# Converting half of a later stage's weights one stage earlier, and passing them through DRAM

## The chip, the cores and the metric

The kernel runs on one core of a Trainium2 chip. The metric is the time of one execution on the device in microseconds (us), the median of several runs. The core's engines are TensorE (PE, with its weight loads shown as PEld), VectorE (DVE), ScalarE (ACT), GpSimd (POOL) and SyncE (SP), which issues nearly all DMAs of this kernel. Each engine works its own queue strictly in order.

## The reference, cut to what matters

```python
x = causal_attention(q, k, v, s)        # 4 batches x 8 heads x 576 positions x 64 -> 2304 tokens x 512
r = maximum(x @ w_in, 0)                # 512 -> 2048          first MLP
x = (s * (r * r) + b) @ w_out           # 2048 -> 512
h = maximum(maximum(x @ w1, x @ w2), x @ w3)   # 512 -> 768 each   second MLP
out = h @ w_out2                        # 768 -> 512
```

The inputs of the second MLP (w1, w2, w3, w_out2) arrive in 64-bit floats. Every product is worked out from operands that are split in a high and a low part ("hi", "lo"), by three TensorE matmuls (L247, L248, L249 of the kernel before).

## The kernel before, in words

There are four stretches.

**Attention and A, 0 to about 345 us.** Attention for 20 jobs runs beside the first half of the first MLP's hidden units ("A"). A goes through eight pieces of tokens, (b, hf) with 320 columns (hf 0) or 256 (hf 1). For each piece come eight "up" products (by `f`, four chunks of 512 inputs each), a relu on DVE (L985), a square and a high part on ACT (L989, L236), a low part on POOL (L243), then four "down" products `e` in two pairs, each left by DVE (`leave`, L1041) into a tile `ya` that SP stores to DRAM (`y0_d`). The attention results (`x_copy`, L614, on DVE) are split for A and also stored to DRAM (`x_d`).

**A alone, about 345 to 432 us.** Attention has ended; the down products of piece (2,0) and the pieces (2,1), (3,0) and (3,1) are left. Until `begin_2` the up and down products share two PSUM banks (ring `mm`); from `begin_2` on there are eight (`mm8`). `begin_2` also frees the attention's memory, so that SP can load the weights of the second half (`wb_in`, `wb_out`, eight loads of 512 KB each, from a DRAM copy `wb_d` that was made earlier) and the first inputs `xs` (`load_x`, from `x_d`; two buffers, split by ACT L1078 and DVE L1080 into `xbh`, `xbl`).

**B, about 432 to 644 us.** The second half of the hidden units, in six groups of 384 tokens: eight up products, relu, square, hi, lo (`gbh`, `gbl`), four down products. `leave` (L1072) adds the first half's result `y0` and writes a tile `y` (ring of two), which SP stores to `y_d`. Beside it the weights of the second MLP are converted, in six "quads": (matrix i, half kk) for w3, w2 and w1. A quad is four pieces of 128 x 384. Each piece is loaded (`wst`, 384 KB, ring of three), scaled on ACT (L1115) and rebuilt as a 32-bit float by four operations and an addition on DVE (L1120, L1122, L1124, L1126, L1102); then come the sums of Strassen's method (`ts`, ring of two), and seven high parts on ACT and seven low parts on DVE (L1099) into the tiles `sw`. The converted w3 is stored to DRAM (21 stores of 256 KB) so that its tile can take w1.

**Stage 3, about 644 us to the end.** The second MLP by the seven products of the Strassen-Winograd method, for four groups of tokens (halves of 320 or 256 columns) and nine units each (three weights times three column blocks `p`). The operand tiles `ty` are made from `y_d` (loads `bl`, shifts on ACT, sums on DVE with the ring `ts`). The weights of w3 are loaded from DRAM again for each unit (`load_s`, L1272, 84 loads of 256 KB, five buffers, shown as `rest`; DRAM tensor `s_d`). When a group is done, the last products (`last`, L247 to L249 on `wf` and `h`, 512 columns) are copied out of PSUM by ACT (`store`, L1372) into the one tile `o` (shown as `rest`), and SP stores it to `out`.

A planner (`Plan`) puts all steps in order when the program is built, from needs, rings of buffers, priorities and its own costs. On the chip each engine then works through its list in that order: a step that waits holds all that stand behind it on its engine, and SP's DMA issues too are such a list.

The lines that set when a quad's piece may start, before:

```python
            g, f = divmod(int(z * PACE_S), NB)       # PACE_S = 1.7, NB = 8
            start = needs + [("middle_2",), ("after", ("upb", g, 0, f, 0))]
```

`middle_2` comes when A's last step is done; `("upb", g, 0, f, 0)` is B's up product f of group g.

## Time and profile before

| | |
|---|---|
| median of three runs | 937.21 us (934.38, 937.21, 939.47) |
| the profiled execution: its time, its span | 938.2 us, 936.4 us |
| mean granted TensorE clock, of full speed | 0.978 |
| busy share: PE, PEld, DVE, ACT, POOL | 95%, 89%, 68%, 54%, 36% |

The span runs from the first to the last recorded instruction; the 1.8 us between it and the time lie around it. A busy share is over the whole span. Times below are microseconds from the span's start. A row of a timeline gives start, duration, engine, line, operation, written tile and read tiles, and in brackets how long the engine had been idle before and what released it. The program's names in rows are those of the trace, where some DRAM tensors and tiles go by a shared name: `y_d` stands for `y_d` and `y0_d`, `rest` for all that is cut from one area in stage 3.

### The profile page before, as it was taken

What the parts mean: (1) busy time and instruction counts of PE and PEld (TensorE: products, weight loads), DVE (VectorE), ACT (ScalarE), POOL (GpSimd) and SP (SyncE); (2) the same over time, 40 slices, a digit from 0 to 9 for tenths busy, and PEclk for the clock granted to TensorE, in tenths of its full rate; (3) what the DMA queues carried; (4) which work ended last, traced back from release to release, by engine and by line L of the source; (5) the groups of instructions that cost most, each with busy time, mean ns of one, the idle gap of its engine ahead of it and who ended that gap; (6) DMA issues with size and microseconds to landing.
All of it is one profiled execution on the core that took longest, in us unless ns stands there. A gap on an engine that the chain in (4) does not pass through costs nothing.

```text
span 936.4 us, 17708 instructions
## 1 busy us (share of the span) xinstructions
PE 891.6 (95%) x6088; PEld 829.6 (89%) x6088; DVE 636.0 (68%) x1623; ACT 505.1 (54%) x1320; POOL 340.4 (36%) x388
## 2 busy tenths in 40 slices
PE   4899899999999999999999999998999999999996
PEld 4677798988888999999999899998998898998995
DVE  7698978887788422224975977948995575765570
ACT  4688699999877733232452553555344344233231
POOL 3344457656554243222331331233233232342220
PEclk8699999999999999999999999999999999999999
DMA  7446365775664101912369244235342343242331
GB/s 237 135 142 193 120 194 184 213 221 159 198 192 160 43 25 55 380 40 91 120 192 280 90 148 138 93 102 186 119 151 87 113 142 117 81 131 94 113 102 45
DMA packets 96841, 131.72 MB, mean 141 GB/s; under 512 B 9200, under 2 KB 61680, under 8 KB 96752
## 3 DMA queue, kind: packets, MB, share of 16 engines
q1 hardware_dynamic: 96656, 130.45, 43.9%
q8 instruction: 48, 0.79, 0.3%
q14 instruction: 41, 0.34, 0.1%
q10 hardware_dynamic: 96, 0.15, 0.0%
HBM read 97.21 MB, written 33.36 MB: 139 GB/s over the span
## 4 chain that ended last, share of the span: by engine, by line
PE 46%; DVE 8%; DMA 7%; issue 3%; ACT 2%; POOL 1%; SPq 0%; ACTq 0%; DVEq 0%; POOLq 0%
PE mm L247 15%; PE mm L248 15%; PE mm L249 15%; DMA wst<-in_moe_w_dram 2%; DMA xs<-x_d 1%; DVE g L985 1%; DMA out_dram<-rest 1%; DVE sw L1099 1%; DMA wb_in<-wb_d 1%; DMA rest<-s_d 1%; DMA y<-y_d 1%; DVE wst L1126 1%; DVE bl L1122 1%; PE px L609 1%; DVE wst L1124 1%
## 5 line engine op out<-in xcount | busy, mean ns | idle before, releaser
L989 ACT ACTIVATE g<-g 128x384 f32<-128x384 f32 (+2 forms) x112 | 53.5, 478 | 115.6 <-DVE g L985 115.5
L1302 DVE TENSOR_TENSOR rest<-mm,rest 128x320 f32<-128x320 f32 (+1 forms) x156 | 70.2, 451 | 58.8 <-ACT rest L1329 42.2
L243 POOL TENSOR_TENSOR gbl<-g,gbh 128x384 fp32r<-128x384 f32 x48 | 55.7, 1161 | 144.4 <-ACT gbh L236 139.1
L247 PE MATMUL mm<-ty,sw 128*128 128x320 f32 (+1 forms) x336 | 99.8, 297 | 4.7 <-ACT rest L1372 2.9
L248 PE MATMUL mm<-ty,sw 128*128 128x320 f32 (+1 forms) x336 | 99.7, 297 | 0.7 <-DVE ty L1099 0.7
L249 PE MATMUL mm<-ty,sw 128*128 128x320 f32 (+1 forms) x336 | 99.4, 296 | 0.0
L590 PE MATMUL pt<-ident,pp 128*128 128x128 f32 x480 | 80.7, 284 | 15.0 <-ACT pt L236 10.7
L985 DVE TENSOR_SCALAR g<-mm 128x384 f32<-128x384 f32 (+2 forms) x112 | 55.3, 495 | 54.8 <-PE mm L249 48.8
L549 ACT ACTIVATE pp<-pp,mn 128x192 f32<-128x192 f32 (+4 forms) x160 | 88.8, 559 | 2.8 <-DVE mn L543 2.7
L243 POOL TENSOR_TENSOR set<-raw,set 64x1152 fp32r<-64x1152 f32 x24 | 65.1, 2712 | 62.9 <-ACT set L472 45.5
L243 POOL TENSOR_TENSOR ga<-g,ga 128x320 fp32r<-128x320 f32 (+1 forms) x64 | 53.8, 843 | 87.6 <-ACT ga L236 84.6
L247 PE MATMUL mm<-xhi,wa_in 128*128 128x320 f32 (+1 forms) x256 | 79.6, 311 | 1.3 <-DVE ya L1041 1.3
L247 PE MATMUL mm<-ga,wa_out 128*128 128x320 f32 (+2 forms) x256 | 80.0, 312 | 0.1
L236 ACT ACTIVATE pt<-pt 128x256 f32<-128x256 f32 (+3 forms) x181 | 72.7, 428 | 11.9 <-PE pt L590 10.7
L249 PE MATMUL mm<-ga,wa_out 128*128 128x320 f32 (+2 forms) x256 | 76.4, 298 | 2.7 <-DVE wa_out L291 2.7
L590 PEld LDWEIGHTS pt<-ident,pp 128*128 128x128 f32 x480 | 56.9, 143 | 24.8 <-ACT pt L236 12.4
L248 PE MATMUL mm<-ga,wa_out 128*128 128x320 f32 (+2 forms) x256 | 76.3, 298 | 0.9 <-POOL ga L243 0.8
L248 PE MATMUL mm<-xlo,wa_in 128*128 128x320 f32 (+1 forms) x256 | 75.8, 296 | 0.2 <-POOL xlo L243 0.2
L543 DVE CUSTOM_DVE_ANT_0 pp<-late_keys,ps 64x64 f32<-64x64 f32 (+4 forms) x160 | 63.2, 420 | 18.7 <-PE ps L532 11.1
L1102 POOL TENSOR_TENSOR rest<-rest 128x320 f32<-128x320 f32 (+1 forms) x48 | 40.8, 857 | 96.7 <-DVE rest L1302 61.7
L249 PE MATMUL mm<-xhi,wa_in 128*128 128x320 f32 (+1 forms) x256 | 75.8, 296 | 0.0
L248 PE MATMUL mm<-gbl,wb_out 128*128 128x384 f32 (+1 forms) x192 | 66.2, 345 | 4.2 <-POOL gbl L243 4.2
(218 smaller groups left out, 2778.1 us busy)
## 6 DMA issues: line engine op xcount, KB each, us to landing
rest<-s_d SPq DMA_DIRECT2D x84, 256.0 KB, 3.1
wst<-in_moe_w_dram SPq DMA_DIRECT2D x24, 384.0 KB, 3.6
raw<-in_q_dram SPq DMA_DIRECT2D x24, 288.0 KB, 4.2
raw<-in_k_dram SPq DMA_DIRECT2D x24, 288.0 KB, 3.3
wb_d<-wbs SPq DMA_DIRECT2D x21, 256.0 KB, 2.5
s_d<-sw SPq DMA_DIRECT2D x21, 256.0 KB, 3.2
xs<-x_d SPq DMA_DIRECT2D x24, 192.0 KB, 3.7
y<-y_d SPq DMA_DIRECT2D x24, 192.0 KB
```

The costliest lines, as they stand in the source:

```text
L236: nc.scalar.activation(dst, src, AF.Copy, scale=1.0 if scale is None else scale)
L243: ENGINES[on].tensor_tensor(dst, a, b, op=ALU.subtract)
L247: nc.tensor.matmul(ps, lhs[0], rhs[0], start=first, stop=False)
L248: nc.tensor.matmul(ps, lhs[0], rhs[1], start=False, stop=False)
L249: nc.tensor.matmul(ps, lhs[1], rhs[0], start=False, stop=last)
L543: nc.vector.tensor_tensor_reduce(out=pp[j][i][:n, k0:k1], in0=late_keys[:n, a:a + k1 - k0], in1=ps_.pop((job.n, u, j))[:n, :k1 - k0], scal ...
L549: nc.scalar.activation(p[:n, :w], p[:n, :w], AF.Exp, bias=mns[job.n, j][:n, i:i + 1], scale=-1.0, accum_out=sums[job.n % 2][:n, j, i:i + 1])
L590: nc.tensor.transpose(pt[:, c - c0, :], pp[j][i][:, c * P:(c + 1) * P], ident)
L985: nc.vector.tensor_scalar(st["g", f], st["u", f][:, :n], 0.0, None, op0=ALU.max)
L989: nc.scalar.activation(st["g", f], st["g", f], AF.Square)
L1102: ENGINES[on].tensor_tensor(dst, a, b, op=ALU.add)
L1302: add(key(name), "DVE", dve_ps(n), prio(), pr(x) + needs, lambda: nc.vector.tensor_tensor(dst(), ps(x), tmp(z), op=ALU.add))
```

## The change

- Three of the six quads, (w3, kk 0), (w3, kk 1) and (w2, kk 0), are converted while A runs alone: their loads may go from `begin_2` on, as A's matmul steps pass certain `marks`. Their high and low parts go to a ring of ten tiles `sd` in memory that later holds `wb_out`, and from there to DRAM (21 stores of 384 KB, tensors `s_d`). (w2, kk 0) is loaded back into `sw` at `middle_2` by seven loads. The other three quads stay in B, with `PACE_S` 3.2 in place of 1.7.
- `begin_2` no longer waits for the last copies of the attention, whose tiles move to a pool of their own (`axp`). So it comes earlier; the eight banks come later, by a step of their own (`banks_2`) behind the last `x_copy`.
- The loads of `wb_in` keep their place behind `begin_2`; those of `wb_out` wait for `middle_o`, when all 21 stores from `sd` are issued.
- `load_s` in stage 3 reads its 256 KB from the `s_d` tensors as they were stored by quad. A run of bytes without a gap on the DRAM side is now 128 elements (512 bytes); it was 512 elements (2 KB).
- B's result tile `y` no longer has a ring of its own but takes the ring `ts` of two, which the Strassen sums of both B and stage 3 use. `y0` takes tiles of `axp`.
- `store` copies into the ring `wst` of three tiles in place of the single `o`, and the DMA to `out` is a step of its own on SP.
- `h` and `tmp` tiles are housed elsewhere, without another operation.

```diff
-WO = ((0, 1, 2), (3, 4), (5, 6, 7))
-PACE_S = 1.7
+WO = ((0, 1, 2), (3, 4, 5), (6, 7))
+SD = (4, 4, 2)
+PACE_S = 3.2
...
-        if att:
+        if att and key[0] not in ("copy_rb", "x_copy", "x_hi", "x_lo"):
             attention.append(key)
...
     def begin_2():
-        phase[0] = 2
         right.close()
...
+    def middle_o():
+        tiles = [late["rwo"].tile([P, 2, len(fs), DM], F32R, name=f"wb_out{z}", tag=f"wo{z}") for z, fs in enumerate(WO)]
...
+    def banks_2():
+        phase[0] = 2
+
+    add(("banks_2",), "", 0.0, 0, [("after", ("x_copy", job.n, hf)) for job in jobs for hf in job.halves], banks_2)
...
-            y = late["sp"].tile([P, G2], F32, name="y", tag=tag("y"))
+            y = late["st2"].tile([P, G2], F32, name="y", tag=tag("ts"))
...
-        nc.sync.dma_start(late["swp"][z].bitcast(F32), s3_d[i // 3][x])
+        p = i // 3
+        nc.sync.dma_start(late["swp"][z].rearrange("p (k n) -> p k n", n=P).bitcast(F32), s_d[1][x][:, :, p * P:(p + 1) * P])
...
+    def save_s(q, x):
+        nc.sync.dma_start(s_d[q[0] - 1][x][:, 2 * q[1]:2 * q[1] + 2], sds[q, x].bitcast(F32))
+
+    def load_sw(kk, x):
+        nc.sync.dma_start(late["sw"][1][:, x, :, kk, :].bitcast(F32), s_d[0][x][:, 2 * kk:2 * kk + 2])
+
+    def window(y):
+        return lambda x: [("begin_2",), ("after", marks[int((4 * y + x) * len(marks) / 15)])]
...
+    STAGED = ((2, 0), (2, 1), (1, 0))
+    for y, (i, kk) in enumerate(STAGED):
+        convert_quad(y, i, (w1, w2, w3)[i], kk, window(y))
...
     def store(g, j):
-        o = late["o"]
+        o = late["st2"].tile([P, DM], F32, name="o", tag=tag("wst"))
...
-            add(("store", g, j), "ACT", act_ps(DM), next_prio(FIRST), [("last", g, j, f)], store, g, j, take=[("o", [("store", g, j)])])
+            add(("store", g, j), "ACT", act_ps(DM), next_prio(FIRST), [("last", g, j, f)], store, g, j, take=[("wst", [("out", g, j)])])
+            add(("out", g, j), "SP", (1, DM), next_prio(FIRST), [("store", g, j)], leave_o, g, j)
```

The order of TensorE's work is the same in both kernels, and the other engines' orders agree up to `begin_2`. Three places show what moves.

DVE, from the attention's last `x_copy` of 320 columns to the relus of piece (2,1), before (`ya<-mm` are the four leaves of piece (2,0)):

```order
L614 TENSOR_TENSOR x_0_4923<-px,rb_4914 128x320
L1041 TENSOR_SCALAR ya<-mm,s_sb 128x320 x4
L985 TENSOR_SCALAR g<-mm 128x256 x8
L614 TENSOR_TENSOR x_1_5188<-px,rb_4739 128x256
L1041 TENSOR_SCALAR ya<-mm,s_sb 128x256
```

The same stretch after the change:

```order
L616 TENSOR_TENSOR x_4940<-px,rb 128x320
L1087 TENSOR_TENSOR xbl_4938<-xs_4936,xbh_4937 128x384
L1087 TENSOR_TENSOR xbl_4944<-xs_4942,xbh_4943 128x384
L1043 TENSOR_SCALAR ya<-mm,s_sb 128x320
...
L1087 TENSOR_TENSOR xbl_4989<-xs_4987,xbh_4988 128x384
L1106 TENSOR_TENSOR sd_4926<-bl,sd_4926 128x384
L1087 TENSOR_TENSOR xbl_5009<-xs_5007,xbh_5008 128x384
L1127 TENSOR_SCALAR bl<-bl 128x384
L1129 SCALAR_TENSOR_TENSOR bl<-wst,bl 128x384
L1131 TENSOR_SCALAR wst<-bl 128x384
L1133 SCALAR_TENSOR_TENSOR wst<-wst 128x384
L1043 TENSOR_SCALAR ya<-mm,s_sb 128x320
```

The third leave of the piece, the last row, now stands behind the splits of all four input chunks and behind most of two pieces of a quad.

SP's DMA issues there, after the change:

```order
L1069 DMA xs_4936<-x_d 128x384
L1069 DMA xs_4942<-x_d 128x384
L1113 DMA wst<-in_moe_w_dram 128x384
L628 DMA x_d<-x_4940 128x320
L1059 DMA wb_in<-wb_d_72 128x2x512
L1059 DMA wb_in<-wb_d_73 128x2x512
L1059 DMA wb_in<-wb_d_74 128x2x512
L1059 DMA wb_in<-wb_d_75 128x2x512
L1059 DMA wb_in<-wb_d_76 128x2x512
L1069 DMA xs_4987<-x_d 128x384
L1113 DMA wst<-in_moe_w_dram 128x384
L1044 DMA y_d<-ya 128x320
```

The third input chunk (`xs_4987`, read by the third `xbl`) is issued behind five loads of `wb_in`; the fourth comes in the row after these. Before, the same sequence, without the `wst` loads, stood some 25 us later, where A had eight banks.

DVE at the passage from B to stage 3 (`y` are leaves of B's last group, `ts` and `ty` the first operands of stage 3), before:

```order
L1072 SCALAR_TENSOR_TENSOR y<-mm,s_sb,y_7973 128x384
L285 TENSOR_SCALAR wst<-wsa 128x256 x2
L1072 SCALAR_TENSOR_TENSOR y<-mm,s_sb,y_7987 128x384
L1099 TENSOR_TENSOR ts<-bl 128x320
L287 SCALAR_TENSOR_TENSOR wst<-wst 128x256
L1099 TENSOR_TENSOR ts<-bl,ts 128x320
```

The same place after the change:

```order
L1079 SCALAR_TENSOR_TENSOR y<-mm,s_sb,y_7839 128x384
L1106 TENSOR_TENSOR ty<-bl,ty 128x320
L1079 SCALAR_TENSOR_TENSOR y<-mm,s_sb,y_7843 128x384
L1106 TENSOR_TENSOR ts<-bl,ts 128x320
...
L1079 SCALAR_TENSOR_TENSOR y<-mm,s_sb,y_7971 128x384
L286 TENSOR_SCALAR wst<-wsa 128x256
L282 SCALAR_TENSOR_TENSOR wsa<-wst,wsa 128x256
L1079 SCALAR_TENSOR_TENSOR y<-mm,s_sb,y_7987 128x384
L1106 TENSOR_TENSOR ts<-bl 128x320
L288 SCALAR_TENSOR_TENSOR wst<-wst 128x256
L1106 TENSOR_TENSOR ts<-bl,ts 128x320
```

The order is nearly the same, but `y` and `ts` now take turns on the same two tiles: a `ts` that follows a `y` in a tile has to wait until SP has stored that `y`. In the upper four rows the second `ts` of kk 0 (`t2`) has also moved: it now follows both leaves of the first pair, which it preceded.

## Rows read from the trace of the kernel before

**Rows 1.** The page's busy times, shares of the span and instruction counts

```profile
PE 891.6 (95%) x6088; PEld 829.6 (89%) x6088; DVE 636.0 (68%) x1623; ACT 505.1 (54%) x1320; POOL 340.4 (36%) x388
```

**Rows 2.** Windows of B: busy (x) PE, PEld, DVE, ACT, POOL; clock, DMA, GB/s

```profile
440.00:460.00 20.00, 19.71 (x113) 19.25 (x112) 19.86 (x38) 12.56 (x32) 10.67 (x15) 1.00 0.30 95
460.00:480.00 20.00, 20.00 (x117) 20.00 (x116) 13.21 (x30) 7.00 (x15) 3.76 (x3) 1.00 0.58 175
480.00:500.00 20.00, 18.19 (x102) 17.40 (x101) 16.11 (x29) 9.07 (x19) 6.00 (x5) 1.00 0.84 246
520.00:540.00 20.00, 17.77 (x88) 16.39 (x87) 19.86 (x37) 9.99 (x22) 5.86 (x5) 0.91 0.36 113
580.00:600.00 20.00, 19.30 (x111) 18.88 (x110) 19.93 (x36) 12.32 (x26) 9.42 (x8) 1.00 0.29 90
```

**Rows 3.** What PE waited for in the whole run: us, times, longest

```profile
PE mm L248 <- POOL gbl L243: 4.2, 6, 1.1
PE mm L247 <- ACT rest L1372: 2.9, 2, 1.5
PE mm L249 <- DVE wa_out L291: 2.7, 1, 2.7
PE mm L247 <- DMA rest<-s_d: 0.9, 2, 0.6
```

**Rows 4.** PE alone behind the wait of 2.7 us: busy (x), clock, DMA, GB/s

```profile
109.00:113.00 4.00, 3.72 (x16) 0.58 0.13 44
```

**Rows 5.** Windows of A alone: all of it, and where PE waited

```profile
345.00:425.00 80.00, 79.01 (x590) 77.95 (x591) 19.20 (x41) 23.59 (x55) 21.09 (x27) 1.00 0.41 144
388.00:394.00 6.00, 6.00 (x43) 6.00 (x42) 2.54 (x6) 3.85 (x9) 2.23 (x3) 1.00 1.05 388
394.00:400.00 6.00, 5.01 (x29) 4.00 (x28) 1.97 (x4) 3.79 (x9) 4.38 (x6) 1.00 0.81 302
```

**Rows 6.** The chain in A alone: start, us, the load of the last `xs`

```profile
379.82 8.37 DMA xs<-x_d
```

**Rows 7.** DMA issues of the whole run: KB each, median us to landing

```profile
xs<-x_d SPq DMA_DIRECT2D x24, 192.0 KB, 3.7
y_d<-y SPq DMA_DIRECT2D x24, 192.0 KB, 1.9
rest<-s_d SPq DMA_DIRECT2D x84, 256.0 KB, 3.1
s_d<-sw SPq DMA_DIRECT2D x21, 256.0 KB, 3.2
vn<-in_v_dram SPq DMA_DIRECT2D x16, 256.0 KB, 3.9
```

**Rows 8.** DVE in order of time: third leave of piece (2,0), first relu of (2,1)

```profile
355.73 0.55 DVE L1041 TENSOR_SCALAR ya<-mm,s_sb 128x320 f32<-128x320 f32 x1 [5.63 <-PE mm L249]
358.08 0.42 DVE L985 TENSOR_SCALAR g<-mm 128x256 f32<-128x256 f32 x1 [0.91 <-PE mm L249]
```

**Rows 9.** DVE's conversion work in B: all on `bl` by window, then two groups

```profile
440.00:625.00 185.00, 84.27 (x147) 0.99 0.48 149
L1126 DVE SCALAR_TENSOR_TENSOR wst<-wst 128x384 f32<-128x384 uint32 x24 | 14.3, 595 | 0.3
L1099 DVE TENSOR_TENSOR sw<-ts,sw 128x384 fp32r<-128x384 f32 x12 | 8.6, 717 | 0.6 <-ACT sw L236 0.6
```

**Rows 10.** From B to stage 3 in order of time, DVE and PE

```profile
632.85 0.48 DVE L1099 TENSOR_TENSOR ts<-bl,ts 128x320 f32<-128x320 f32 x1
633.61 0.62 DVE L1072 SCALAR_TENSOR_TENSOR y<-mm,s_sb,y 128x384 f32<-128x384 f32 x1 [0.28 <-PE mm L249]
...
646.17 0.42 PE L247 MATMUL mm<-ty,sw 128*128 128x320 f32 x1 [1.81 <-ACT ty L236]
```

**Rows 11.** The end in order of time: PE's last matmul, ACT's last store

```profile
928.27 0.39 PE L249 MATMUL mm<-wf,h 128*128 128x512 f32 x1
932.83 0.60 ACT L1372 ACTIVATE rest<-mm 128x512 f32<-128x512 f32 x1 [2.14 <-DMA out_dram<-rest]
```

More of the change, by code (lines that the diff above doesn't have):

```diff
@@ L927, in begin_3 @@
             wf[f] = p3.tile([P, 2, DM], F32R, name=f"wf{f}")
-        for f in (0, PAIRS, 2, 2 + PAIRS):
-            hs[f] = [p3.tile([P, 2 * WIDE], F32R, name=f"h{z}{f}") for z in range(2)]
+        where = {0: (p3, p3), PAIRS: (p3, p3), 2: (p3, p3), 2 + PAIRS: (p3, 1), 1: (0, 0), 1 + PAIRS: (0, 0)}
         space = [[late["rwo"].tile([P, 2 * len(fs) * DM], dt, name=f"rest{z}", tag=f"wo{z}"), 0] for z, (fs, dt) in enumerate(zip(WO, (F32R, F32R, F32)))]
@@ L1094, in fused_kernel @@
     ORDER = (A11, A12, S2, S1, S3, A22, S4)
-    s3_d = [[dram.tile([P, 4 * P], F32, name=f"s3_d{p}_{x}") for x in range(7)] for p in range(PAIRS)]
-    blocks, tss, wsts = {}, {}, {}
+    s_d = [[dram.tile([P, 2 + 2 * i, HALF], F32, name=f"s_d{i}_{x}") for x in range(7)] for i in range(2)]
+    blocks, tss, wsts, sds = {}, {}, {}, {}
+    marks = [k for k in users_a if k[0] in ("mm1", "downa") and (k[:3] == ("downa", 2, 0) or k[1:3] in ((2, 1), (3, 0), (3, 1)))]
     def tsub(dst, a, b, on):
@@ L1144, in both, with seven, convert_quad @@
         return {"DVE": dve(n), "Pool": pool_(n)}
-    def seven(key, n, x, src, dst, prio, needs, k):
-        add((key, *k, x, "hi"), {"ACT": act(n), "DVE": dve_fast(n) - 0.06}, 0, prio(), needs, hi_, lambda: dst(0, x), src)
+    def seven(key, n, x, src, dst, prio, needs, k, **a):
+        add((key, *k, x, "hi"), {"ACT": act(n), "DVE": dve_fast(n) - 0.06}, 0, prio(), needs, hi_, lambda: dst(0, x), src, **a)
         add((key, *k, x, "lo"), both(n), 0, prio(), [(key, *k, x, "hi")], lo_, lambda: dst(1, x), src, lambda: dst(0, x))
-    def convert_quad(y, i, w, kk, where, needs):
+    def convert_quad(y, i, w, kk, at):
+        staged = (i, kk) in STAGED
         q = (i, kk)
@@ L1158, in convert_quad @@
             z = 4 * y + x
-            g, f = divmod(int(z * PACE_S), NB)
             k = lambda s: ("q", *q, "c", x, s)
             p0 = FILL + 1000 + 10 * z
-            start = needs + [("middle_2",), ("after", ("upb", g, 0, f, 0))]
-            add(k("load"), "SP", (1, 2 * HALF), p0, start, q_load, q, x, w[c * P:(c + 1) * P, n0:n0 + HALF], take=[("wst", [k("whole")])])
+            add(k("load"), "SP", (1, 2 * HALF), p0, at(x), q_load, q, x, w[c * P:(c + 1) * P, n0:n0 + HALF], take=[("wst", [k("whole")])])
             add(k(0), "ACT", act(HALF), p0, [k("load")] + ([("q", *q, "c", x - 1, 0)] if x else []), q_scale, q, x, take=[("bl", release[v]) for v in range(4)] if x == 0 else [])
@@ L1168, in convert_quad, with d @@
         whole = lambda *xs: [("q", *q, "c", x, "whole") for x in xs]
-        d = lambda hl, x: where()[:, x, hl, kk, :]
+        def d(hl, x):
+            if not staged:
+                return late["sw"][i][:, x, hl, kk, :]
+            if (q, x) not in sds:
+                sds[q, x] = late["sd"][plan.slot("sd")[1]]
+            return sds[q, x][:, hl]
         p0 = FILL + 1000 + 10 * (4 * y + 3) + 6
@@ L1177, in convert_quad, with split @@
         ts = lambda n: (lambda: tss[q, n])
-        seven("q", HALF, A11, blk(0), d, pr_, whole(0) + needs, q)
+        def split(x, src, needs):
+            seven("q", HALF, x, src, d, pr_, needs + ([] if staged else [("middle_2",)]), q, take=[("sd", [("save_s", *q, x)])] if staged else ())
+            if staged:
+                add(("save_s", *q, x), "SP", (1, 2 * HALF), pr_(), done(x), save_s, q, x)
+        split(A11, blk(0), whole(0))
         add(("q", *q, "s3"), both(HALF), 0, pr_(), whole(0, 2), lambda on: (ts_tile((q, S3), HALF), tsub(tss[q, S3], blocks[q, 0], blocks[q, 2], on)),
@@ L1194, in fused_kernel @@
[L1194 to L1203 removed]
+        split(A12, blk(1), whole(1))
@@ new lines, in fused_kernel @@
+    STAGED = ((2, 0), (2, 1), (1, 0))
+    for y, (i, kk) in enumerate(STAGED):
+        convert_quad(y, i, (w1, w2, w3)[i], kk, window(y))
+    add(("middle_o",), "", 0.0, 0, [("after", ("save_s", i, kk, x)) for i, kk in STAGED for x in range(7)] + [("begin_2",)], middle_o)
+    for x in range(7):
+        add(("q", 1, 0, x, "in"), "SP", (1, 2 * HALF), FILL + 1500, [("middle_2",), ("save_s", 1, 0, x)], load_sw, 0, x)
+    for y, (i, kk) in enumerate(((1, 1), (0, 0), (0, 1))):
+        convert_quad(3 + y, i, (w1, w2, w3)[i], kk, stage_b_(y))
@@ L1321, in unit @@
             for x in ORDER:
-                add(("ls", g, i, x), "SP", (1, 4 * P), next_prio(FIRST), [("begin_3",), ("save_s", p, x)], load_s, g, i, x, take=[("sp", [("pr", g, i, x)])], delay=0.5)
+                add(("ls", g, i, x), "SP", (1, 4 * P), next_prio(FIRST), [("begin_3",)] + [("save_s", 2, kk, x) for kk in range(2)], load_s, g, i, x, take=[("sp", [("pr", g, i, x)])], delay=0.5)
         reader = {A11: key("p1"), A12: key("c11"), S2: key("u2"), S1: key("c22"), S3: key("u3"), A22: key("get", "c21"), S4: key("get", "c12")}
```

67 lines of the change are left out of this document (31 added, 36 removed).

## The prediction, made before the changed kernel ran

> **What bounds the kernel now.** I read the page's busy times first: TensorE is busy for 95% of the span [rows 1]. Its work and its order stay the same, so the change can only take away or add idle time and slow stretches of TensorE. The table of waits then tells which of these exist. The ones that the change touches are waits for `gbl` in B, for `store` (L1372) at the seams of stage 3, and for the loads of w3 [rows 3]. A busy share hides part of B's loss, so I count matmuls in windows instead. An undisturbed window of 20 us holds 117 (0.171 us each); the disturbed ones hold 113, 102, 88 and 111 [rows 2]. That is 4 + 15 + 29 + 6 = 54 matmuls, or **9.2 us lost in B**. In three of these four windows DVE is busy for 19.9 of 20 us; in the fourth (480 to 500, DVE 16.1) the DMAs are at 0.84 [rows 2]. The relus come late because they stand in DVE's queue among the conversions; the `gbl` that TensorE waits for is the end of that chain.
>
> Part of such a loss is clock. In the window at 520 to 540 the mean granted clock is 0.91 [rows 2]. After the wait of 2.7 us near 109 us [rows 3], the next 4 us were granted 0.58 on average, so a large part at the lower level of 1.2 GHz instead of 2.4; that cost 4 x 0.42 = 1.7 us [rows 4]. The two waits for `store`, of at most 1.5 us, brought no such dip that a window shows. I add 1.7 us to a single wait of 2.7 us or more.
>
> **1. The entry into A alone: +6.0 us (bounds +1.3 and +7.5).** `begin_2` now comes as soon as the attention's last product is read, near 345 us, so SP issues five loads of `wb_in` of 0.6 us each from about 345.2, and the third `xs` behind them at about 348.3. Before, an `xs` that was issued behind such loads took 8.37 us from issue to landing [rows 6], where the median is 3.7 [rows 7]. By 8.37 it lands at 356.7; ACT and DVE split it in about 0.5 us each, by 357.5, and the fourth is split right behind it. What is queued behind these splits on DVE is the third leave of piece (2,0): four more operations of a quad come first, 2.4 us by their means, so it starts near 360 and ends 0.55 later. Before, it ran at 355.73 [rows 8]. The first up product of piece (2,1) needs its bank: with 12 matmuls of 0.12 us before the relu at 358.08 [rows 8] it began near 356.5, and now begins near 360.8. So TensorE stands 4.3 us, and the dip of 1.7 follows. With the median landing of 3.7 the leave ends near 357.7 and the wait is 1.3 us without a dip. The upper bound adds 1.5 us for the fourth `xs`, should it land that much later. I take the high price since the row with the same queue in front of it is the nearest.
>
> The Trainium skill ("DMA: Bandwidth & Descriptors", queues, rings and completion order) says that on each DMA engine descriptors are consumed in ring order, so that a small load waits for the big ones issued ahead of it; it speaks against this change, and the trace agrees (8.37 against 3.7 us). Bytes alone would let the `xs` land some 3 us sooner (5 x 512 KB at the 388 GB/s of [rows 5] is 6.8 us from 345.2), with a wait near 2 us and no dip: the sum below would be 4 us lower.
>
> **2. The same wait in its old place: -2.0.** Between 394 and 400 us TensorE did 29 matmuls, against 43 in the 6 us ahead [rows 5]: 14 x 0.14 = 2.0 us. DVE stood there behind the same kind of late `xs`; with eight banks open it cost only this. It goes.
>
> **3. Conversions beside A: +2.5 (0 and +6).** All six quads cost DVE 84.3 + 14.3 + 8.6 = 107 us [rows 9], so three cost 53.6. From 345 to 425 us DVE was busy for 19.2 of 80 us [rows 5]; with 53.6 more it is 73, a share of 0.91. This is the load at which B lost time: 9.2 us over 200. For 80 us at that rate it is 3.7; at the rate of the worst window (5 us in 20 [rows 2]) it would be far more, which is a rival below. A's pieces are shorter (256 and 320 columns) but after 370 us eight banks let relus come late. I take 2.5.
>
> **4. B: -7.3 (-9.2 and -4).** Half of its conversions are gone, and the rest is spread over 1.9 times as many steps; DVE's load in 440 to 625 us falls by about 50 of 185 us. I leave 1.9 us of the 9.2 for the start of B, where `wb_out`, the seven loads of (w2, kk 0) and the next quad's `wst` are all issued after about 425 us, and DVE's first operation on a late `wst` would stand ahead of a relu.
>
> **5. From B to stage 3: +4.0 (+1.5 and +6).** `y` and `ts` share two tiles. The first leave of B's last pair is at 633.61 [rows 10]; its store takes 1.9 us [rows 7], so the second leave waits until about 636.5 and `t2` until about 639.2, the landing of the second leave's store. Before, `t2` ran at 632.85 [rows 10]. Behind it on DVE stand the `ty` parts and the conversion of the last weights, whose end releases a `wst` load on SP, behind which the last three `bl` loads are queued. These come some 3.5 us later, and with them the `ty` that TensorE already waited 1.81 us for at 646.17 [rows 10]. The next pair then delays `t1` and `t2` once more, by the same 1.9 us each, partly in parallel. Lower bound: only the second pair's two stores count, less the slack between them.
>
> **6. `load_s` in 512-byte runs: +2.0 (0 and +7).** The fifth buffer frees late, so the last two loads of each of 12 units have 2.9 us (halves of 256, four parts of 0.72) or 3.5 (320). They land after 3.1, and TensorE waited 0.9 in total, twice [rows 3, 7]. The nearest row, the stores of the same tensors in 512-byte pieces, has 3.2; a load in 512-byte pieces from an input has 3.9 [rows 7]. The first adds at most 0.1 to each of six units, the second 0.8 to six and 0.4 to six, 7 us. I take 2, nearer to the first. The same page of the Trainium skill (specifications) puts the smallest transfer at full rate at 512 bytes, by which this term is nothing; the row of 3.9 disagrees, though that queue was busier.
>
> **7. Results through three tiles: -7.0 (-7 and -4).** The two waits at the seams, 2.9 us [rows 3], have the single `o` as their cause, which waits for its DMA. At the end, ACT copies the last result at 932.83, held by the DMA before it, while TensorE's last matmul ends near 928.7 [rows 11]. With a free tile this copy starts 4.1 us earlier, and so does the end.
>
> The new places of `h` and `tmp` have the same operations; I cost them at nothing, since no step gets another wait that I could find except through `ts`.
>
> **The sum**: 6.0 - 2.0 + 2.5 - 7.3 + 4.0 + 2.0 - 7.0 = -1.8, from 938.2 us of the profiled execution to 936.4. That execution lies 1.0 us above the median of 937.21; from the median it is **935.4 us**.
>
> **The rivals.**
> - *The new waits stay small (faster).* If the `xs` land in about 5 us and `t2`'s delay is absorbed, terms 1, 3, 5 and 6 shrink to 2 + 1.5 + 2 + 0.5, and with -2, -7.3 and -7 the sum is -10: **927 us**. For it: the wait of 8.37 had six loads of `wb_in` and not five issued ahead of it, and DMAs at 1.05 behind it [rows 5]. Against it: the rows with the same queue.
> - *DVE saturates beside A (slower).* If the 80 us with DVE at 0.91 lose half of what the worst window of B lost (2.5 us in 20), term 3 is +10 and the time **943 us**. It decides if DVE has no gap of several us between 362 and 422. For it: three of four bad windows had DVE at 19.9 of 20 [rows 2]. Against it: the window of B with DVE at 13.2 of 20 lost nothing [rows 2], and from about 370 us on eight banks are open.
> - *512-byte loads bind stage 3 (slower).* At 3.9 us term 6 is +7: **940.5 us**, and more where loads queue behind each other.
> - *B keeps its losses*, since they come from loads and stores of w3, as the window at 480 to 500 with the DMAs at 0.84 may mean [rows 2]: term 4 is -4, **939 us**.
>
> **How the numbers follow.** About 0.5% (4.7 us) is what a measurement of this kernel can tell from no change. My forecast, all terms near their values, has 0.40 and holds 931 to 940. The small waits have 0.30, the saturated DVE 0.17, the 512-byte loads 0.08, B's kept losses 0.05. Faster means below 932.5: all of the first rival and 0.07 of the forecast, 0.37. Slower means above 941.9: 0.17 of the DVE case, 0.04 of the loads, 0.03 of the forecast, 0.24. The same: 0.39. The range reaches from the first rival to the saturated DVE, and 2 to 3 us beyond, since term 4 may be -9.2 and term 5 +6: 925 to 946.
>
> **What would show it.** Term 1: a gap of TensorE of 3 to 6 us near 357 and a lower clock after it. 2: none at 394 to 400. 3: more than 73 us of DVE in the same 80, and few missing matmuls. 4: windows of B with 117 matmuls and DVE below 15 of 20. 5: `t2` behind a `y` store, and a first wait in stage 3 above 4 us. 6: landing times of `load_s` and waits for them. 7: no waits for `store`, and the last copy within 0.5 us of the last matmul. The forecast is wrong above all if the gap of term 1 is missing, or if matmuls are missing all through A.

## The result, and where the time went

The changed kernel takes **946.96 us** (median of 11 runs, 941.36 to 949.39) against 937.21 for the kernel before (11 runs by now, 934.38 to 940.55): a ratio of **1.0093, 95% interval 1.0068 to 1.0119**. The ratio is worked out from all runs of both kernels; the two medians alone would give 1.0104. It is slower by about 1%, where 935.4 was forecast in a range of 925 to 946. Its profiled execution took 948.19 us.

TensorE's busy share is the same as in [rows 1], and so is its count of matmuls:

```profile
span 946.2 us, 17754 instructions
...
PE 894.9 (95%) x6088; PEld 831.6 (88%) x6088; DVE 643.1 (68%) x1623; ACT 506.6 (54%) x1323; POOL 333.3 (35%) x385
```

Since TensorE does the same matmuls in the same order in both kernels, the start of the same matmul can be compared in the two traces. The difference at some places, worked out from the starts in the two timelines (not a view of the profile itself):

```
place (first matmul after it)                before     after   difference
end of attention                              344.5     346.0       +1.5
A, piece (2,1), first relu's product          357.6     365.3       +7.7
A, behind the wait that was at 396            399.0     405.0       +6.1
B begins                                      432.7     440.9       +8.2
B, first down products begin                  451.0     459.2       +8.2
B, two us later in the kernel before          452.8     467.9      +15.1
B, last down products                         640.6     646.9       +6.3
stage 3, a dozen products in                  647.7     658.4      +10.7
first seam, ahead of it and behind it   715.1, 731.0  727.5, 741.7  +12.5, +10.7
second seam, ahead and behind           865.0, 871.4  878.3, 883.2  +13.4, +11.9
last products                                 926.2     939.9      +13.7
end of the span                               936.4     946.2       +9.8
```

The places where the forecast put a loss or a gain all show; three things come out of the table that it did not have in size: the start of B (+6.9), the creep through stage 3 (the difference grows by 6.2 outside the seams), and 1.5 us that lie ahead of all that the change touches and differ from run to run.

A seam is where stage 3 goes from one group of tokens to the next; the two in the table are those that held a wait for `store` before.

The waits of TensorE that answer to [rows 3], after the change (us, times, longest): `store` and the waits of B for `gbl` are nearly gone; the third leave `ya` of piece (2,0), the first `gbh` of B, `ty` at the start of stage 3 and the loads of w3 have taken their place.

```profile
PE mm L248 <- DVE ya L1043: 6.2, 2, 4.9
PE mm L248 <- ACT ty L237: 3.8, 2, 2.8
PE mm L248 <- ACT gbh L237: 3.6, 1, 3.6
...
PE mm L248 <- DMA rest<-s_d: 2.7, 8, 0.6
...
PE mm L248 <- DVE rest L1338: 1.9, 4, 0.5
PE mm L249 <- DVE ty L1106: 1.4, 1, 1.4
PE mm L249 <- POOL gbl L244: 1.1, 2, 0.9
```

Windows of the changed kernel, with the columns of [rows 2] (us; PE, PEld, DVE, ACT, POOL busy and instructions; clock; DMA share; GB/s), from A to the start of stage 3:

```profile
345.00:425.00 80.00, 74.61 (x555) 73.67 (x552) 60.53 (x119) 33.08 (x73) 18.26 (x21) 0.98 0.68 234
...
440.00:460.00 20.00, 20.00 (x118) 19.49 (x116) 6.43 (x12) 4.90 (x13) 5.44 (x8) 1.00 1.02 365
460.00:480.00 20.00, 15.30 (x75) 14.36 (x75) 12.70 (x25) 8.28 (x21) 6.17 (x8) 0.83 0.40 136
...
480.00:500.00 20.00, 20.00 (x117) 20.00 (x116) 14.57 (x28) 10.16 (x21) 8.15 (x7) 1.00 0.30 99
520.00:540.00 20.00, 20.00 (x116) 20.00 (x116) 18.99 (x33) 12.49 (x26) 9.20 (x8) 1.00 0.23 79
580.00:600.00 20.00, 20.00 (x117) 20.00 (x116) 14.71 (x26) 10.22 (x21) 7.89 (x7) 1.00 0.30 99
640.00:660.00 20.00, 14.63 (x74) 13.54 (x73) 14.20 (x36) 8.57 (x21) 0.88 (x1) 0.83 0.63 193
```

From 345 to 425 us DVE is busy for 60.5 of 80 us, where the forecast's sign was more than 73, and 35 matmuls are missing against [rows 5]. B's later windows now hold their full 116 to 118 matmuls, as forecast, one of them with DVE busy for 19.0 of 20 us, where less than 15 was forecast. So a nearly full DVE need not cost a matmul. B's second window holds 75, with DVE busy for only 12.7 of 20 us: that loss is not one of a full DVE. The window ahead of it shows the DMAs at 1.02 and DVE at 6.4 of 20.

**The entry into A alone**, DVE in order of time (start, us, line, operation, what it waited for):

```profile
353.13 0.56 DVE L1109 TENSOR_TENSOR bl<-bl,wst 128x384 f32<-128x384 f32 x1
358.18 0.56 DVE L1087 TENSOR_TENSOR xbl<-xs,xbh 128x384 fp32r<-128x384 f32 x1 [4.49 <-ACT xbh L1085]
358.65 0.55 DVE L1106 TENSOR_TENSOR sd<-bl,sd 128x384 fp32r<-128x384 f32 x1
360.09 0.56 DVE L1087 TENSOR_TENSOR xbl<-xs,xbh 128x384 fp32r<-128x384 f32 x1 [0.88 <-ACT xbh L1085]
...
362.42 0.54 DVE L1043 TENSOR_SCALAR ya<-mm,s_sb 128x320 f32<-128x320 f32 x1
```

and TensorE's next matmul with the two microseconds of PE alone that follow (us, busy, clock, DMA share, GB/s):

```profile
363.01 0.58 PE L248 MATMUL mm<-xhi,wa_in 128*128 128x256 f32 x1 [4.91 <-DVE ya L1043]
...
363.00:365.00 2.00, 1.99 (x9) 0.50 1.03 408
```

DVE stands idle for 4.5 us ahead of the third `xbl`, and the leave at 362.42 stands behind four of the quad's operations. That is the mechanism of term 1 as it was worked out, with the low clock behind it (0.50 is the lower of the two levels, 1.2 GHz).

**The start of B**, DVE:

```profile
444.59 0.48 DVE L1043 TENSOR_SCALAR ya<-mm,s_sb 128x256 f32<-128x256 f32 x1 [8.73 <-DMA y_d<-ya]
448.06 0.48 DVE L1043 TENSOR_SCALAR ya<-mm,s_sb 128x256 f32<-128x256 f32 x1 [2.99 <-DMA y_d<-ya]
...
455.25 0.36 DVE L1127 TENSOR_SCALAR bl<-bl 128x384 int32<-128x384 int32 x1 [3.43 <-ACT bl L1122]
...
456.12 0.55 DVE L987 TENSOR_SCALAR g<-mm 128x384 f32<-128x384 f32 x1
...
462.53 0.36 DVE L1127 TENSOR_SCALAR bl<-bl 128x384 int32<-128x384 int32 x1 [3.23 <-ACT bl L1122]
462.80 0.55 DVE L987 TENSOR_SCALAR g<-mm 128x384 f32<-128x384 f32 x1
```

and SP's issues there (start, us over all, count):

```profile
449.00 0.53 SPq L1214 DMA_DIRECT2D sw<-s_d  x1
449.58 0.61 SPq L1113 DMA_DIRECT2D wst<-in_moe_w_dram  x1
450.25 3.80 SPq L1214 DMA_DIRECT2D sw<-s_d  x6
454.09 1.28 SPq L1113 DMA_DIRECT2D wst<-in_moe_w_dram  x2
```

First the last leaves of A wait for tiles `ya` whose stores stand behind loads of `wb_out`. Then the second `wst` is issued behind six loads of `sw` (384 KB each) and the relu at 462.80 stands on DVE behind the operation that waits for it. TensorE waits 3.58 us for the `gbh` that comes of it, at 463.6; between 364 us and that point it had no wait above 0.5 us, so the waits for `ya` had not held it.

**From B to stage 3**, DVE: the second leave waits for the store of the first, `t2` for that of the second, and `t1` of the next pair for the next.

```profile
642.88 0.62 DVE L1079 SCALAR_TENSOR_TENSOR y<-mm,s_sb,y 128x384 f32<-128x384 f32 x1 [1.61 <-DMA y_d<-y]
645.48 0.49 DVE L1106 TENSOR_TENSOR ts<-bl,ts 128x320 f32<-128x320 f32 x1 [1.98 <-DMA y_d<-y]
...
655.50 0.49 DVE L1106 TENSOR_TENSOR ts<-bl 128x320 f32<-128x320 f32 x1 [1.68 <-DMA y_d<-y]
```

**Stage 3's loads** (KB, median us to landing) land after 4.2 us, where [rows 7] has 3.1:

```profile
rest<-s_d SPq DMA_DIRECT2D x84, 256.0 KB, 4.2
```

**The end**: the last copy follows the last matmul within 0.1 us, as against [rows 11].

```profile
942.01 0.39 PE L250 MATMUL mm<-wf,rest 128*128 128x512 f32 x1
...
942.49 0.60 ACT L1406 ACTIVATE o<-mm 128x512 f32<-128x512 f32 x1 [0.83 <-PE mm L250]
```

### The profile page after: what moved, and what is told of

Same layout as the page of the kernel before. It is cut to its first block, busy times and chain, and to the rows that moved or that the text cites. A ratio compares the mean times of both kernels' runs of the same rounds, so it can differ in the third digit from the quotient of the medians.

```text
span 946.2 us, 17754 instructions
## 1 busy us (share of the span) xinstructions
PE 894.9 (95%) x6088; PEld 831.6 (88%) x6088; DVE 643.1 (68%) x1623; ACT 506.6 (54%) x1323; POOL 333.3 (35%) x385
## 4 chain that ended last, share of the span: by engine, by line
PE 52%; DMA 7%; DVE 3%; issue 1%; SPq 1%; ACT 1%; POOL 1%; DVEq 0%; ACTq 0%; POOLq 0%
PE mm L248 17%; PE mm L249 17%; PE mm L250 17%; DMA rest<-s_d 3%; DMA wst<-in_moe_w_dram 1%; DMA xs<-x_d 1%; DMA y_d<-y 1%; DMA y_d<-ya 1%; PE px L611 1%; DVE rest L1338 1%; SPq L1059 0%; SPq L1214 0%; PE pt L592 0%; DVE g L987 0%; POOL gbl L244 0%
## 5 line engine op out<-in xcount | busy, mean ns | idle before, releaser
L244 POOL TENSOR_TENSOR gbl<-g,gbh 128x384 fp32r<-128x384 f32 x48 | 53.8, 1122 | 144.7 <-ACT gbh L237 139.2
L545 DVE CUSTOM_DVE_ANT_0 pp<-late_keys,ps 64x64 f32<-64x64 f32 (+4 forms) x160 | 63.1, 419 | 19.6 <-PE ps L534 11.6
L248 PE MATMUL mm<-gbh,wb_out 128*128 128x384 f32 (+1 forms) x192 | 65.7, 342 | 3.6 <-ACT gbh L237 3.6
L248 PEld LDWEIGHTS mm<-ty,sw 128*128 128x128 f32 x336 | 64.2, 191 | 4.5 <-ACT ty L237 4.3
```

What stands on the lines that cost most here:

```text
L244: ENGINES[on].tensor_tensor(dst, a, b, op=ALU.subtract)
L248: nc.tensor.matmul(ps, lhs[0], rhs[0], start=first, stop=False)
L545: nc.vector.tensor_tensor_reduce(out=pp[j][i][:n, k0:k1], in0=late_keys[:n, a:a + k1 - k0], in1=ps_.pop((job.n, u, j))[:n, :k1 - k0], scal ...
```

## The experiments

Theory: four places lose time, each for a reason of its own (the entry, the start of B, the passage to stage 3, the loads of w3). Ratios are against the kernel before on the same chip; 0.1% is 0.94 us. Each time is the median of 6 to 12 executions. A difference to the change in us is that of the two ratios.

**1. The loads of (w2, kk 0) later.**

```diff
-[("middle_2",), ("save_s", 1, 0, x)], load_sw, 0, x)
+[("middle_2",), ("save_s", 1, 0, x), ("after", ("upb", 2, 0, x, 0))], load_sw, 0, x)
```

Expected: 

> The changed kernel with one edit: the seven loads that bring (w2, kk 0) back wait for steps of B's third group instead of being issued at B's start. Theory (the first loads of B's own quads land late because 2.7 MB stand ahead of them, and relus stand behind them on DVE and ACT): the two waits of TensorE near 460 us (3.6 and 0.9 us) and the low clock behind them go for the greater part, 4 to 6 us less than the changed kernel's 947.0, so 941 to 943. Rival (the start of B is late because the loads of wb_out stand ahead of the last stores of ya and so hold the last leaves of A): the waits stay, 946 to 948.

Measured: 939.22 us, ratio 1.0032 (1.0008 to 1.0057), 5.7 us less than the change. The wait of 3.58 us for `gbh` is gone; this is left:

```profile
PE mm L249 <- POOL gbl L244: 1.8, 2, 1.3
```

The theory holds for the start of B: loads that nobody needs for 200 us stood ahead of loads that the relus' engine waited for. The rival, the loads of `wb_out` ahead of the stores of `ya`, falls: those waits are still there in this run,

```profile
443.29 0.48 DVE L1043 TENSOR_SCALAR ya<-mm,s_sb 128x256 f32<-128x256 f32 x1 [8.94 <-DMA y_d<-ya]
```

and yet TensorE loses only 1.5 us there.

**2. wb_in as a block behind the xs.**

```diff
-[("begin_2",) if z < len(side) // 2 else ("middle_o",)] + ...
+([("begin_2",), ("after", ("xb_lo", 0, NE - 1))] if z < len(side) // 2 else [("middle_o",)]) + ...
```

Expected: 

> The changed kernel with one edit: the eight loads of wb_in are issued only behind the split of the fourth input chunk of B's first group. Theory (the third and fourth xs wait in the DMA queue behind five loads of wb_in, and the third leave of piece (2,0) stands behind their splits on DVE): the wait of 4.9 us near 358 us and the 1.7 us of low clock behind it go, 5 to 7 us less than 947.0, so 940 to 942. Rival (the leave is held by the quad's operations ahead of it, whose own loads are late): the xs land in about 4 us, but a wait of 2 us or more remains and the gain is at most 3 us.

Measured: 946.11 us, ratio 1.0120 (1.0086 to 1.0155). Neither theory nor rival held in full: the wait for the leave goes, as the theory said, but the time does not. The third leave came at 356.85 instead of 362.42, and the first up products of (2,1) 5.7 to 7.0 us earlier in the trace than in the changed kernel. But the next `wst` now lands behind the block, and relus wait for it on DVE:

```profile
363.29 0.36 DVE L1127 TENSOR_SCALAR bl<-bl 128x384 int32<-128x384 int32 x1 [2.22 <-ACT bl L1122]
```

and TensorE waits for relus:

```profile
PE mm L248 <- DVE g L987: 4.6, 2, 2.8
```

So the xs were the cause of that leave's delay, but not of the loss: in this run the `wst` behind 4 MB of loads brings one.

**3. y written in place.** `evac` writes over `y0`, which gets a third tile.

```diff
-            y = late["st2"].tile([P, G2], F32, name="y", tag=tag("ts"))
-            nc.vector.scalar_tensor_tensor(y, ps, s_sb[:, 0:1], y0s[e], op0=ALU.mult, op1=ALU.add)
+            y = y0s[e]
+            nc.vector.scalar_tensor_tensor(y, ps, s_sb[:, 0:1], y, op0=ALU.mult, op1=ALU.add)
```

Expected: 

> The changed kernel with one edit: B's result is written in place over y0, which gets three tiles, so that y no longer takes turns with the Strassen sums on two tiles. Theory (t1 and t2 of stage 3 wait on DVE until SP has stored a y): no waits of ts for y_d<-y, and the first waits of stage 3 (1.0, 2.9 and 1.4 us, with low clock behind them) fall back to the 1.8 and 0.8 us of before, 3.5 to 5 us less than 947.0, so 942 to 943.5. Rival (the passage is set by the last weight loads and bl loads, as the 1.8 us of before may show): the time stays within 1.5 us of 947.

Measured: 943.02 us, ratio 1.0081 (1.0049 to 1.0113). By the ratio alone it can't be told from the change. In the trace no leave or `ts` waits for a store of `y` there, and the first products of stage 3 stand 1.8 us better against the changed kernel behind the passage than ahead of it. The waits for `ty` are 2.9 us on ACT's and 0.5 on DVE's, in place of 3.8 and 1.4:

```profile
PE mm L248 <- ACT ty L237: 2.9, 2, 1.5
...
PE mm L249 <- DVE ty L1107: 0.5, 1, 0.5
```

By this run some 40% of the +4.4 of the passage comes from the shared tiles; the table behind the experiments has more traces. What is left was not tried. In this run ACT waits 5.1 us for a load `bl` there, and DVE 4.3 us for a weight of the last products (L277) that ACT does behind it, which the theory did not have.

**4. w3's sums by column block.** Runs of 2 KB for the loads, 512 bytes for the stores, of which there are two for each sum and quad of w3 in place of one (not shown here).

```diff
...
-        nc.sync.dma_start(late["swp"][z].rearrange("p (k n) -> p k n", n=P).bitcast(F32), s_d[1][x][:, :, p * P:(p + 1) * P])
+        nc.sync.dma_start(late["swp"][z].rearrange("p (k n) -> p k n", n=P).bitcast(F32), s_d[1][x][:, p])
```

Expected: 

> The changed kernel with one edit: w3's sums lie in DRAM by column block, so that each of the 84 loads of stage 3 reads runs of 2 KB again; the short runs are on the side of the stores from sd. Theory (the 512-byte loads land after 4.2 us instead of 3.1 and cost TensorE 6 us over stage 3): landing near 3.1 us, issue 0.32 us, 5 to 6 us less than 947.0, so 941 to 942. Rival (stage 3 loses time because the planner gave DVE, ACT and POOL another order there, as the waits for DVE at L1338 may show): the landing falls but the time by at most 2.5 us, and the waits for DVE stay.

Measured: 941.9 us, ratio 1.0065 (1.0039 to 1.0091). SP's issue of one load fell from 0.52 to 0.32 us, the landing from 4.2 to 3.8, not to 3.1. The waits for DVE at L1338 are gone, and TensorE gains 5.4 us on the changed kernel between its 663 and its 924 us. So the creep through stage 3 does come from these loads, the waits for DVE among it; the time of the whole shows 2.6 us of it, with the two intervals overlapping. The landing did not fall as the theory had it, so how a run's length delays TensorE is not shown by it.

**5. wb_in one by one.**

```diff
+    steps_a = [k for k in users_a if k[0] in ("mm1", "downa") and (k[:3] == ("downa", 2, 0) or k[1:3] in ((2, 1), (3, 0), (3, 1)))]
...
+([("begin_2",), ("after", steps_a[int((z + 2) * len(steps_a) / 11)])] if z < len(side) // 2 else [("middle_o",)]) + ...
```

Expected: 

> The changed kernel with one edit: the eight loads of wb_in are issued one by one between A's matmul steps, about one in 9 us, instead of together. Theory after the run that held them back as a block (any load behind that block is late, and where it isn't an xs it is the quad's wst, with relus behind it on DVE and ACT): neither the wait of 4.9 us near 358 us nor the two of 1.9 and 2.8 us near 365 and 374 us of that run; 5 to 7 us less than the changed kernel, a ratio to the kernel before of 1.002 to 1.004. Rival (DVE is too full beside A, and a wait appears there wherever the loads stand): the sum of waits between 345 and 380 us stays above 3 us and the ratio above 1.007.

Measured: 946.79 us, ratio 1.0097 (1.0066 to 1.0128): no gain. The wait at the entry is gone and TensorE is 6.7 us ahead of the changed kernel there; by 405 of the changed kernel's time it has lost 3.6 of these again, and by 463 another 1.6. The time is the rival's, the place is not: between 345 and 380 us TensorE has no wait at all, and the loss comes later. The windows below show where.

**6. Three result tiles alone, on the kernel before.**

```diff
-        o = late["o"]
+        o = late["st2"].tile([P, DM], F32, name="o", tag=tag("wst"))
...
+            add(("out", g, j), "SP", (1, DM), next_prio(FIRST), [("store", g, j)], leave_o, g, j)
```

Expected: 

> The kernel before with one part of the change alone: results leave through the three tiles of the wst ring, the DMA to out being a step of its own. Theory: the two waits for L1372 (1.5 and 1.3 us) go and the last copy comes 4.1 us earlier, 7 us in all, a ratio of 0.9925. Rival (the waits at the seams hide others, of the first operands of the next group): only the 4.1 us at the end, a ratio of 0.9955.

Measured: 927.65 us, ratio **0.9902** (0.9866 to 0.9938), 9.2 us less. No wait for `store` is left, and the last copy starts 0.1 us behind the last matmul's end. Its trace has 7.4 us of it at the two seams and the end; the rest is within the interval. This one part would have made the kernel faster; all the rest of the change together costs 18 us on top of it (1.0093 - 0.9902, of 937).

**7. Five edits at once** (1, 3, 4, 5, and `wb_out` behind the second leave of A's last piece). The last is new, shown against number 5:

```diff
-else [("middle_o",)]) + ...
+else [("middle_o",), ("after", ("leavea", B - 1, 1, 1))]) + ...
```

Expected: 

> The changed kernel with five edits at once: wb_in issued one by one, wb_out behind the second leave of A's last piece, the loads of (w2, kk 0) in B's third group, y written in place over y0, and w3's sums in DRAM by column block. Theory (the four places where the changed kernel lost time are independent and the conversions themselves do fit beside A): the gains add up, 6 + 6 + 2.5 + 4 us, about 18 us less than the changed kernel: a ratio to the kernel before of 0.989 to 0.993. Against the kernel before with three result tiles alone it says whether moving the quads brings anything: by the theory 1 to 4 us. Rival (the losses overlap, since a wait that goes lets the next one take its place): a ratio above 0.995.

Measured: 928.92 us, ratio 0.9930 (0.9900 to 0.9961). The gains do add up for the greater part, 15 us of the 18 expected. But the kernel is not faster than number 6: against its trace, moving three quads brings B some 9 us and costs as much in A and at B's start.

**8. The same with two quads beside A**, their pieces spread over the same stretch and so a third thinner; (w2, kk 0) is converted in B and no longer passes through DRAM.

```diff
-PACE_S = 3.2
+PACE_S = 2.6
...
-    STAGED = ((2, 0), (2, 1), (1, 0))
+    STAGED = ((2, 0), (2, 1))
```

Expected: 

> The kernel with all five edits, but only the two quads of w3 are converted beside A (their pieces spread over the same stretch) and four stay in B, in steps of 2.6. Theory now (DVE and the engines behind it are too full beside A with three quads: of the 9 us that leave B some 5 come back between 390 and 425 us): with a third less beside A that loss falls to 1 to 2 us while B still loses little, a ratio to the kernel before of 0.987 to 0.990, 3 to 5 us less than with three quads. Rival (the loss beside A comes from loads that stand behind others, not from DVE's load): a ratio of 0.992 to 0.995, as with three.

Measured: 920.18 us, ratio **0.9814** (0.9781 to 0.9848), the fastest kernel of this study. The window of A in which number 7 lost its time, in four kernels, each fence one kernel. The changed kernel, number 5, number 7 and number 8:

```profile
390.00:430.00 40.00, 39.52 (x288) 39.08 (x286) 33.06 (x64) 19.61 (x44) 11.38 (x13) 1.00 0.49 165
```

```profile
390.00:430.00 40.00, 36.89 (x254) 35.40 (x253) 32.53 (x63) 19.83 (x45) 12.55 (x15) 0.96 0.58 198
```

```profile
390.00:430.00 40.00, 36.60 (x245) 34.57 (x244) 32.38 (x61) 18.01 (x41) 10.96 (x13) 0.91 0.64 208
...
392.00:396.00 4.00, 2.00 (x6) 1.11 (x6) 3.97 (x8) 2.80 (x6) 1.82 (x2) 0.82 0.68 229
```

```profile
390.00:430.00 40.00, 40.00 (x308) 40.00 (x307) 21.43 (x43) 14.42 (x33) 10.88 (x13) 1.00 0.59 176
```

Number 7 does 245 matmuls where number 8 does 308; where they are missing, DVE is busy for 3.97 of 4 us, and ACT stands idle for 1.65 us until DVE has done a relu (392.46). But ahead of this, at 383.39, DVE had itself been idle for 3.90 us until ACT had the next `wst`: so DVE's mean load alone does not explain the loss; pieces that come late and then close together may be part of it. With two quads DVE has 21 of 40 us to do there and nothing is missing. The third quad's loads, stores and ACT work left this stretch with its DVE work, so this run does not tell which of them it is. The changed kernel did 288, with the same DVE work as number 7: it had stood 6 us at the entry, and its conversions had come further meanwhile (ACT begins on the seventh and eighth piece 31 and 35 matmuls earlier, by TensorE's count, than in number 7).

**9. All edits, but wb_in and wb_out where the change had them** (edits 1, 3 and 4 alone).

Expected: 

> The kernel with all five edits less two: wb_in and wb_out are issued where the changed kernel has them, so that the wait of 5 to 7 us near 355 us is back. Theory (while TensorE waits there, DVE works off conversions that would make TensorE wait later, so the losses overlap): the time is within 3 us of the kernel with all five edits, a ratio of 0.992 to 0.996, and few matmuls are missing between 390 and 425 us. Rival (the wait costs its 6 us in full): a ratio of 0.998 to 1.001.

Measured: 933.35 us, ratio 0.9960 (0.9936 to 0.9985). The wait of 5.6 us at the entry is back, and of the 6 to 8 us by which its trace falls behind that of number 7 there, 5.6 are made up again between 402 and 406 us, while 283 matmuls stand in the window of 390 to 430. The losses overlap; the time is 0.3% above number 7, within what both intervals allow.

**10 and 11. w3's sums in blocks without gaps**, three stores for each: on the changed kernel (the diff), and on number 8.

```diff
-        nc.sync.dma_start(s_d[q[0] - 1][x][:, 2 * q[1]:2 * q[1] + 2], sds[q, x].bitcast(F32))
...
+            for p in range(PAIRS):
+                nc.sync.dma_start(s3_d[p][x][:, 2 * q[1]:2 * q[1] + 2], sds[q, x][:, :, p * P:(p + 1) * P].bitcast(F32))
```

Expected (10): 

> The changed kernel with w3's sums in DRAM as the kernel before had them: each load of stage 3 reads one block of 256 KB without gaps, written in three stores per sum and quad. In the run with 2 KB runs the DRAM rows of one load still lay 6 KB apart, and it landed after 3.8 us, not 3.1. Theory (the place of the rows in DRAM costs the remaining 0.6 us): landing near 3.2, waits for these loads below 1 us in all, 1 to 2 us less than that run, a ratio of 1.004 to 1.006. Rival (the loads land late because more of them are in flight together in this kernel's order): landing stays at 3.7 to 3.9 and the ratio at 1.006 to 1.008.

Expected (11): 

> The kernel with two quads beside A and the five edits, with the same block layout of w3's sums. Theory: as above, 1 to 2 us less than with column blocks 6 KB apart, a ratio of 0.979 to 0.981. Rival: no difference, 0.981 to 0.983; or more, if the 42 shorter stores in place of 28 delay loads beside A.

Measured: 945.19 us, ratio 1.0105 (1.0070 to 1.0140), and 923.61 us, ratio 0.9873 (0.9838 to 0.9908). The theory fell. Number 10 lies above what theory and rival had and can't be told from the change; number 11 is slower than number 8 (the intervals overlap by 0.1%), as the end of its rival allowed. The loads land after 3.6 and 3.8 us, where number 8, with its rows 6 KB apart, has

```profile
rest<-s_d SPq DMA_DIRECT2D x84, 256.0 KB, 3.1
```

so the place in DRAM does not set it. Number 11 loses some 5 us against number 8 near 422 to 430 us, where relus' low parts come late (`ga`, 1.4 us of waits and the clock behind them); its 42 stores in place of 28 are the only edit that bears on that stretch. What makes these loads land between 3.1 and 4.0 us (number 7) at equal length of run stays open.

**The same places in all traces.** How far TensorE's start moves against the kernel before in each stretch of the table above, in us, worked out from the starts in each timeline (not a view of the profile). "Ahead" is the start of the run to the end of attention, "stage 3" is without the two seams, "seams" has these and the end.

```
run                     ahead  A alone  B's start      B  passage  stage 3  seams
the changed kernel       +1.5     +6.7       +6.9   -8.8     +4.4     +6.2   -7.1
1  sw loads later        -2.2     +8.9       +1.5   -8.4     +4.3     +4.2   -7.4
2  wb_in as a block      +1.1     +8.5       +8.1   -8.2     +5.5     +4.8   -7.4
3  y in place            -1.2     +8.8       +6.4   -8.5     +2.6     +6.9   -7.4
4  2 KB runs             +0.4     +6.8       +7.2   -8.7     +5.9     +0.6   -7.0
5  wb_in one by one      +1.0     +5.0       +7.5   -8.0     +5.5     +7.1   -7.4
6  three tiles alone     -2.5     -0.3       +0.2   +0.9     -0.6     -0.1   -7.4
7  five edits            -4.4     +6.7       +2.2   -9.2     -0.5     -1.1   -7.3
8  two quads             +0.5     -2.0       -0.1   -8.8     +2.1     -1.5   -7.0
9  edits 1, 3, 4         +0.1     +8.5       +2.0   -8.9     +2.3     +0.8   -7.1
10 block layout          -1.6     +9.7       +6.9   -8.1     +6.0     -0.8   -7.1
11 block, two quads      +1.0     +3.7       -0.1   -8.7     +2.1     -1.7   -7.2
```

Three columns fall into groups by one edit each. B's start costs 6.4 to 8.1 us where the seven loads of `sw` stand there and 2.2 at most where they don't. The passage costs 4.3 to 6.0 us where `y` shares the tiles of `ts` and 2.6 at most where it doesn't; the kernels without the sharing differ in other edits too. Stage 3 loses 4.2 to 7.1 us with loads in runs of 512 bytes and 0.8 at most with 2 KB. A alone is the one that does not part so cleanly: 6.7 to 9.7 us with the entry's wait (number 2, with its own waits, lies among them), 5.0 and 6.7 without it (5 and 7), and -2.0 and 3.7 with two quads. Number 10 has lost in A and in the passage what it gained in stage 3.

## Why the prediction was wrong

By its own terms, with what the two traces of the table above show (profiled executions, as the forecast's sum was):

- **Term 1, the entry: +6.0 forecast, +6.2 found** (1.5 to 7.7). The wait was 4.91 us, and the clock behind it 0.50. That the size came out so near is in part luck: the third `xs` was issued 2.2 us later than worked out (350.5), and ACT began on it 7.1 us later, where 8.37 was assumed. The row of 8.37 is that of the fourth `xs`, with seven loads of `wb_in` ahead of it and not six; after the change the fourth took 7.3. The Trainium skill ("DMA: Bandwidth & Descriptors", queues, rings and completion order) has the rule that spoke against this place, and the trace agrees with it (7.3 us behind the loads, against a median of 3.4).
- **Term 2, the old wait: -2.0 forecast, -1.6 found.**
- **Term 3, conversions beside A: +2.5 forecast, +2.1 found**, which is luck. Without the entry's wait the stretch from the end of attention to B still costs 5.0 and 6.7 us, term 2's gain counted in (runs 5 and 7), and run 8, with two quads, loses nothing there (run 11, with two as well, 3.7). So three quads beside A do cost, as term 3 had it, and more than it had; in the changed kernel the entry's wait hides this. Whether DVE's load or the late `wst` is the cause was not separated. Terms 1 and 3 were added as if independent; they share one loss, so that undoing term 1 alone gains 1.7 and 1.8 us in the two pairs of traces (the change and 5, 9 and 7) and nothing in the time of run 5.
- **Term 4, B: -7.3 forecast, -1.9 found. This step failed first.** The later B gave back 8.8 us (15.1 to 6.3), near the 9.2 that it could. But "I leave 1.9 us of the 9.2 for the start of B" was far too little: the start cost 6.9. The mechanism was named (a late `wst` with a relu behind it), and the 1.9 us were what was left over, not worked out. The rows for it were there: the seven loads of `sw` are 2.75 MB, 7 us at the 388 GB/s of [rows 5], and relus are due all the while. Run 1 shows it: with these loads later the start costs 1.5 us, although the eight loads of `wb_out`, which the prediction named with them, stay.
- **Term 5, the passage: +4.0 forecast, +4.4 found.** The waits for stores of `y` are there; run 3 gives the tiles some 40% of it, and the table of all traces more: the median passage is 5.5 us with the sharing and 2.1 without. The first waits of stage 3 were at most 2.8 us each, where one above 4 us was forecast. The rest of the passage stays open.
- **Term 6, 512-byte loads: +2.0 forecast, +6.2 found. The second step that failed.** I took the value next to the stores' 3.2 us. The nearest row in kind, the only load in 512-byte pieces, was the one of 3.9, and the landing became 4.2; its bound of +7 was near. Between the rule of the Trainium skill (the same page, specifications: full rate from 512 bytes on) and that row I weighed the rule too highly. Run 4, where runs of 2 KB bring 5.4 us back in stage 3, decides against 512 bytes. But the step from landing to loss is not shown: the median landing was 4.0 us in run 7, in runs of 2 KB and without a loss in stage 3, and 3.9 in run 2, in runs of 512 bytes and with 4.8 us of it. What parts the two groups without exception is SP's time to issue a load, 0.52 against 0.32 us; that it is the cause was not tried.
- **Term 7, three tiles: -7.0 forecast, -7.1 found** (1.7 and 1.5 at the seams, 3.9 at the end), and run 6 shows it by itself (7.4 in its trace).

Terms 4 and 6 are 9.6 us off together; with the 1.5 us ahead of the change and smaller parts that makes the 11.6 between the -1.8 of the sum and the +9.8 of the spans. The rival that came nearest in time was the saturated DVE, 943 us, but it wasn't what happened in the changed kernel. Its sign came, for DVE has no gap above 1.5 us between 362 and 422 us; its loss did not, for from 366 to 441 us TensorE has only three waits of 0.2 to 0.5 us. Losses of 5.0 and 6.7 us appear when the entry's wait is removed (runs 5 and 7).

## What to carry to other kernels

When work is moved, follow its loads, not only its operations: each large block of transfers that the move puts into a queue (weights freed earlier, data parked in DRAM and read back) delays whatever small load is issued behind it, and the cost is that of the operations that stand behind the waiting one on an engine that works in order (here relus behind a conversion's first operation). Put a number on each such queue, bytes ahead over the rate of a busy window, before leaving a remainder by feel. A stall can hide another: the engine behind works ahead while TensorE waits, so one fix alone may show nothing, and how much work a stretch can hold shows only when its stalls are gone; here three quads cost time beside A, and two did in one of the two runs that had them. And a gain that needs none of this, three result tiles in place of one, was worth 9 us by itself, about as much as the move in its best form brought on top of it (number 8 against number 6, 8 us), and more than the move as it was made.
